# Equal distances for tile 0's lent banks, and two token groups of batch 1's q loaded after its v

**Chip, cores, metric.** One core of a Trainium2 chip. The metric is device time in microseconds (us) of one execution; lower is better. All runs named here are at a granted TensorE clock of 0.992 to 1.0.

## The reference, cut to what matters

An efficient attention feeds a two-layer network with a sine in the middle. Everything is f32 at the interface.

```python
q_s = softmax(q, axis=-1)                      # q, k, v: (8 batches, 8 heads, 576 tokens, 64)
k_s = softmax(k, axis=2)                       # over the tokens
kv  = einsum('bhsd,bhse->bhde', k_s, v)
x   = einsum('bhsd,bhde->bhse', q_s, kv)       # -> (4608 tokens, 512)
h   = x @ w_in                                 # (512, 2048)
g   = h + sin(alpha * h)**2 / alpha
out = g @ w_out                                # (2048, 512)
```

## The kernel before

The network runs over nine tiles of 512 tokens; attention of batch b + 1 is laid between the matmuls of tile b. PE is TensorE, DVE is VectorE, ACT is ScalarE, POOL is GpSimd, SP is SyncE, which issues most DMAs. One batch is 576 tokens, kept as J = 9 groups of 64, so tile 1 needs batch 0's last group and seven groups of batch 1; groups 7 and 8 of batch 1 belong to tile 2. In the listings `kvp` is the product of k and v in PSUM, `kbd` the same after its normalization, `xp` the attention output in PSUM and `xT` its bf16 copy, the network's input; the norm of q is a sum, a reciprocal and a product (`qs`, `qn`), and `o` is an output block on its way out.

The first layer's output for one of 16 column blocks (ni) stands in a PSUM bank until ACT has taken its sine and DVE has combined the two. There are four banks for that (`ps_h`), and tile 0 borrows two more from the attention's pool (`wide`):

```python
elif wide and (ni in (4, 5, 9, 10, 14, 15) if t == 0 else ni % 6 in (4, 5)):
    hp = wide()                     # a lent bank
else:
    hp = ps_h.tile([128, MF], F32, name="hp", tag="h")
```

Between tile 0's second layer and tile 1, batch 1 is prepared (cut; `take(os, n)` lets n matmuls of tile 0's second layer go by, four of its 64 also copy out an output block):

```python
take(os, 46)
exp_to(A["qe", 0][:, 8:9], staged["q", 0][:, :, 8:9])
exp_q(1)
load("v", v, 1, halves=True)
load_batch(2)
norm_q8(); norm_q(1, [GP, V]); exp_k(1)
# ... transposes of q (PE), two copies of them (DVE) ...
cast_v(1, [ACT_CP, DVE_CP])                    # f32 -> bf16, half on ACT, half on DVE
nc.scalar.activation(zero, zero, AX.Sin)       # switches ACT's table from Exp to Sin
take(os, 6)
# ... small xp of batch 0's last group; DVE copies it to xT ...
take(os, 2); kv_mm(1, 0, ps_e, split=True); kv_norm(1, 0, 1)
take(os, 2); kv_mm(1, 1, ps_e, split=True); kv_norm(1, 1, 2)
take(os, 1)
# ... xp and its copy to xT for batch 1's groups 0 to 6, then take(os) and tile 1 ...
```

In tile 1's second layer, batch 2 is prepared. SP issues here: the output block's two writes (inside `take`), batch 3's v, then two DMA transposes of batch 2's q.

```python
exp_q(2); exp_k(2)
os = o_stream(1)
take(os, 8)
# ... xp of batch 1's groups 7 and 8, DVE copies it to xT ...
take(os, 8)                          # first output block: DVE copies, SP writes it in two DMAs
norm_q(2, [GP, V])
exp_q(3); exp_k(3)
load("v", v, 3)
q_transpose_dma(2, halves=True)
# ... take(os, 16), kv of batch 2, take(os, 20) ...
# xp of batch 2 (needs the transposed q), tile 2
```

The softmax here doesn't subtract the row's maximum and nothing guards it: scores larger than these inputs give would overflow.

Of the kernel before, what the change touches and what calls it, by code (L numbers as in the profile page):

```python
# [15 lines left out]
F32 = mybir.dt.float32  # L16
BF16 = mybir.dt.bfloat16
AX = mybir.ActivationFunctionType
# [5 lines left out]
def kernel(  # L24
# [40 lines left out]
    ident = singles.tile([128, 128], F32, name="ident")  # L65
    identb = singles.tile([128, 128], BF16, name="identb")
    xT = singles.tile([128, 4, NT], BF16, name="xT")
    win = singles.tile([128, 4, d_ff], BF16, name="win")
    wout = singles.tile([128, nN, dm], BF16, name="wout")
    alpha_rows = singles.tile([nN, 128], F32, name="alpha_rows")  # L70
# [5 lines left out]
    def src_view(t, b):  # L76
        return t[b].rearrange("(i e) (p j) d -> (e p) i (j d)", e=2, j=J)
# [7 lines left out]
    def load(name, t, b, halves=False, eng=nc.sync, gate=None):  # L85

        st = stage.tile([128, 4, J, D], F32, name=f"st_{name}", tag="st")
        for ii in range(2) if gate else ():
            gate(st[:, ii, 0, 0:1], zero)
        view = src_view(t, b)  # L90
        flat = st.rearrange("p i j d -> p i (j d)")
        if halves:
            for ii in range(2):
                eng.dma_start(out=flat[:, ii::2], in_=view[:, ii::2])
        else:
            eng.dma_start(out=flat, in_=view)
        staged[name, b] = st

    def load_batch(b):
        load("q", q, b)  # L100
        load("k", k, b)
        load("v", v, b)
# [6 lines left out]
    def load_wout(c):  # L109
        nc.gpsimd.dma_start(out=wout[:, 4 * c:4 * c + 4, :], in_=wout_v[:, 4 * c:4 * c + 4, :])  # L110
# [4 lines left out]
    def exp_to(dst, src, iis=range(2)):  # L115
        for ii in iis:
            nc.scalar.activation(dst[:, :, ii * 128:(ii + 1) * 128].rearrange("p j (x d) -> p x j d", x=2),  # L117
                                 src[:, ii::2], AX.Exp)

    def exp_q(b):  # L120
        A["qe", b] = att2.tile([128, J, 4 * D], BF16, name="qe")
        exp_to(A["qe", b], staged["q", b])

    def exp_half(name, b, ii, j1=J):
        if ii == 0:
            A[name + "e", b] = att2.tile([128, J, 4 * D], BF16, name=name + "e")
        exp_to(A[name + "e", b][:, 0:j1], staged[name, b][:, :, 0:j1], (ii,))
# [5 lines left out]
    def cast_v(b, engs):  # L133
        vv = vb[b % 2].rearrange("p j (i c) -> p i j c", i=4)
        for ii in range(2):
            engs[ii](vv[:, 2 * ii:2 * ii + 2, :, 0:D], staged["v", b][:, ii::2])  # L136

    def norm_q(b, engs, j1=J):

        qe = A["qe", b][:, 0:j1].rearrange("p j (ii x d) -> p ii j x d", ii=2, x=2)  # L140
        A["qn", b] = qn = att1.tile([128, 2, J, 2 * D], BF16, name="qn")
        qs = small.tile([128, J, 4], F32, name="qs")
        if len(engs) == 1:
            nc.vector.tensor_reduce(qs, A["qe", b].rearrange("p j (i d) -> p j i d", i=4), axis=AXL.X, op=ALU.add)  # L144
            nc.vector.reciprocal(qs, qs)  # L145
        for ii in range(2):
            part = qs[:, 0:j1, 2 * ii:2 * ii + 2]
            if len(engs) == 2:
                nc.vector.tensor_reduce(part, qe[:, ii], axis=AXL.X, op=ALU.add)  # L149
                nc.vector.reciprocal(part, part)  # L150
            engs[ii % len(engs)].tensor_tensor(qn[:, ii, 0:j1].rearrange("p j (x d) -> p j x d", x=2), qe[:, ii],  # L151
                                               part.unsqueeze(3).to_broadcast([128, j1, 2, D]), op=ALU.mult)

    def norm_q8():

        qe = A["qe", 0][:, 8].rearrange("p (i d) -> p i d", i=4)
        qs = small.tile([128, J, 4], F32, name="qs")[:, 0]
        nc.vector.tensor_reduce(qs, qe, axis=AXL.X, op=ALU.add)
        nc.vector.reciprocal(qs, qs)
        nc.vector.tensor_tensor(qe, qe, qs.unsqueeze(2).to_broadcast([128, 4, D]), op=ALU.mult)  # L160

    def kv_mm(b, ii, pool, split=False):

# [22 lines left out]
    def q_tile(b):  # L186
        if ("qT", b) not in A:
            A["qT", b] = att2.tile([128, 2, J, 128], BF16, name="qT")
        return A["qT", b]

    def q_transpose(b, ii, pool, eng):
        tp = pool.tile([128, 16, 128], BF16, name="tp", tag="a")
        q_transpose_ii(b, ii, 0, J, tp)
        eng(q_tile(b)[:, ii], tp[:, 0:J])

    def q_transpose_ii(b, ii, j0, j1, tp):

        for j in range(j0, j1):
            nc.tensor.transpose(tp[:, j - j0], A["qn", b][:, ii, j], identb)
# [35 lines left out]
    def mm_h(t, ni, wide=None, k0=0, k1=4):  # L235

        if ni == 0 and k0 == 0:
            G[t] = gpool.tile([128, nN, MF], BF16, name="g")
        if k0:
            hp = HP[t, ni]  # L240
        elif wide and (ni in (4, 5, 9, 10, 14, 15) if t == 0 else ni % 6 in (4, 5)):
            hp = wide()
        else:
            hp = ps_h.tile([128, MF], F32, name="hp", tag="h")
        HP[t, ni] = hp
        for ki in range(k0, k1):
            nc.tensor.matmul(hp, win[:, ki, ni * 128:(ni + 1) * 128],  # L247
                             xT[:, ki, t * MF:(t + 1) * MF], start=(ki == 0), stop=(ki == 3))
        return hp
# [138 lines left out]
    def take(it, n=1000):  # L388
        for _ in range(n):
            if next(it, 0) == 0:  # L390
                return
# [4 lines left out]
    with ES:  # L396
        def lent():
            return ps_e.tile([128, 2, MF], F32, name="hh", tag="a")[:, 0]

        def load_q8():  # L400
            for ii in range(2):
                load0(nc.sync, "q", q, ii, 8, 9)

        late = {4: load_q8, 6: lambda: load("q", q, 1, halves=True, gate=DVE_CP), 8: lambda: load_wout(2),
                10: lambda: load_wout(3), 13: lambda: load("k", k, 1, halves=True, gate=DVE_CP)}
        for ni in range(nN):
            h_slot(0, ni, "DPPAPPAPPPAPPAPP"[ni], lag, lent)
            flush(lag, 1)
            if ni in late:
                late[ni]()  # L410
        flush(lag, 0)

        accs = [ps_h.tile([128, dm], F32, name="hp", tag="h") for _ in range(4)]
        os = o_quad(0, accs, [DVE_CP, ACT_CP, DVE_CP, ACT_CP])
        take(os, 46)
        exp_to(A["qe", 0][:, 8:9], staged["q", 0][:, :, 8:9])
        exp_q(1)
        load("v", v, 1, halves=True)
        load_batch(2)
        norm_q8()  # L420
        norm_q(1, [GP, V])
        exp_k(1)
        q_transpose(1, 0, ps_e, DVE_CP)
        tp = ps_e.tile([128, 16, 128], BF16, name="tp", tag="a")
        q_transpose_ii(1, 1, 0, J, tp)
        for ii in range(2):
            nc.tensor.transpose(tp[:, J + ii], A["qe", 0][:, 8, ii * 128:(ii + 1) * 128], identb)
        DVE_CP(A["qT", 1][:, 1], tp[:, 0:J])
        DVE_CP(A["qT", 0][:, :, 8], tp[:, J:J + 2])
        cast_v(1, [ACT_CP, DVE_CP])  # L430
        nc.scalar.activation(zero, zero, AX.Sin)
        take(os, 6)
        xp = ps_e.tile([128, 4, P], F32, name="xp", tag="a")
        for c in range(4):
            attn_chunk(0, c, 8, 9, xp[:, c])
        DVE_CP(xT[:, :, 8 * P:9 * P], xp)  # L436
        take(os, 2)
        kv_mm(1, 0, ps_e, split=True)
        kv_norm(1, 0, 1)
        take(os, 2)  # L440
        kv_mm(1, 1, ps_e, split=True)
        kv_norm(1, 1, 2)
        take(os, 1)

        c0 = J * P
        for ii in range(2):
            xp = ps_e.tile([128, 2, 512], F32, name="xp", tag="a")[:, :, 0:7 * P]
            for e in range(2):
                attn_chunk(1, 2 * ii + e, 0, 7, xp[:, e])
            (ACT_CP, DVE_CP)[ii](xT[:, 2 * ii:2 * ii + 2, c0:c0 + 7 * P], xp)  # L450
            take(os, 2)
        take(os)
        load("q", q, 3)
        load("k", k, 3)

        for ki in range(2):
            for ni in range(2):
                mm_h(1, ni, lent, ki, ki + 1)
        for ni in range(nN):
            h_slot(1, ni, SQ[ni], lag, lent)  # L460
            flush(lag, 1)
        cast_v(2, [GP_CP, GP_CP])
        flush(lag, 0)
# [16 lines left out]
    exp_k(2)  # L480
    os = o_stream(1)
    take(os, 8)
    xp = ps_a.tile([128, 4, 2 * P], F32, name="xp", tag="a")
    for c in range(4):
        attn_chunk(1, c, 7, 9, xp[:, c])
    DVE_CP(xT[:, :, (J + 7) * P:2 * J * P], xp)
    take(os, 8)
    norm_q(2, [GP, V])
    exp_q(3)
    exp_k(3)  # L490
# [107 lines left out]
```

## Time and profile before

| what | value | from |
|---|---|---|
| time | 289.31 us median of 4 (289.15 to 289.55) | the runs |
| span in the trace | 287.7 us | the profile |
| PE busy | 273.6 us, 95% | busy shares |
| PE's waits for other engines between 15 and 80 us that are listed | 0.7 + 0.7 + 0.3 us | list of waits |
| tile 1's first layer starts | 47.95 us | timeline |
| tile 1's second layer, start to tile 2's first matmul | 61.76 to 78.33, 16.57 us | timeline |

A matmul of 512 columns is recorded with 379 ns, but the next starts 216 ns later; the records overlap. A wait below about 0.16 us is therefore not seen as idle, and the end of one stage is best read as the start of the next. I compare stages by the starts of their first matmuls. Tile 2's start (start, duration, engine, line, operation):

```profile
78.33 3.62 PE L247 MATMUL hp<-xT,win 128*128 128x512 bf16 x15
```

### The profile page before, as it was taken

What the parts mean: (1) busy time and instruction counts of PE and PEld (TensorE: products, weight loads), DVE (VectorE), ACT (ScalarE), POOL (GpSimd) and SP (SyncE); (2) the same over time, 40 slices, a digit from 0 to 9 for tenths busy, and PEclk for the clock granted to TensorE, in tenths of its full rate; (3) what the DMA queues carried; (4) which work ended last, traced back from release to release, by engine and by line L of the source; (5) the groups of instructions that cost most, each with busy time, mean ns of one, the idle gap of its engine ahead of it and who ended that gap; (6) DMA issues with size and microseconds to landing.
All of it is one profiled execution on the core that took longest, in us unless ns stands there. A gap on an engine that the chain in (4) does not pass through costs nothing.

```text
span 287.7 us, 4238 instructions
## 1 busy us (share of the span) xinstructions
PE 273.6 (95%) x1541; PEld 131.3 (46%) x1569; DVE 189.2 (66%) x285; ACT 226.0 (79%) x319; POOL 81.8 (28%) x77
## 2 busy tenths in 40 slices
PE   2898998999999999999999999999999999999995
PEld 1444454445454445444544454444444444444443
DVE  4957966889958667856776676747674555555412
ACT  4978755999479999899889988998877777777500
POOL 2969420675775571005300440022000000000000
PEclk9999999999999999999999999999999999999999
DMA  7999999935899957129910991115111111111142
GB/s 260 311 200 247 264 395 407 309 150 166 190 181 402 371 185 126 38 45 375 265 34 22 328 311 29 38 39 131 24 39 36 36 36 39 36 36 38 40 109 73
DMA packets 38053, 45.77 MB, mean 159 GB/s; under 512 B 16512, under 2 KB 21392, under 8 KB 38032
## 3 DMA queue, kind: packets, MB, share of 16 engines
q1 hardware_dynamic: 32848, 40.57, 46.2%
q0 software_dynamic: 4992, 4.79, 9.6%
q8 instruction: 12, 0.20, 0.3%
q10 hardware_dynamic: 192, 0.14, 0.2%
q14 instruction: 9, 0.07, 0.1%
HBM read 36.71 MB, written 9.44 MB: 160 GB/s over the span
## 4 chain that ended last, share of the span: by engine, by line
PE 76%; DMA 9%; DVE 5%; ACT 3%; POOL 3%; issue 3%; SPq 0%; POOLq 0%; DVEq 0%; ACTq 0%
PE hp L247 34%; PE op L267 30%; DMA qT<-qn 4%; DMA st_v<-in_v_dram 4%; PE hh L247 2%; PE kvp L170 2%; PE xp L219 2%; POOL qn L151 1%; POOL s L257 1%; ACT s L253 1%; PE warm L328 1%; DMA st_q<-in_q_dram 1%; PE op L568 1%; PE op L247 1%; DVE qs L144 1%
## 5 line engine op out<-in xcount | busy, mean ns | idle before, releaser
L263 DVE SCALAR_TENSOR_TENSOR g<-s,inva_sb,hp 128x512 bf16<-128x512 f32 x130 | 96.3, 746 | 64.4 <-ACT s L255 54.5
L247 PE MATMUL hp<-xT,win 128*128 128x512 bf16 x512 | 129.0, 379 | 0.5
L267 PE MATMUL op<-wout,g 128*128 128x512 bf16 x479 | 121.8, 379 | 1.1 <-issue 0.5
L253 ACT ACTIVATE s<-hp,alpha_sb 128x512 f32<-128x512 f32 x130 | 87.7, 682 | 27.4 <-PE hp L247 25.1
L247 PEld LDWEIGHTS <-win 128*128 128x128 bf16 x576 | 56.2, 98 | 68.2 <-issue 1.2
L267 PEld LDWEIGHTS <-g 128*128 128x128 bf16 x560 | 54.1, 98 | 61.4 <-issue 0.6
L255 ACT ACTIVATE s<-s 128x512 f32<-128x512 f32 x111 | 69.9, 630 | 3.5
L151 POOL TENSOR_TENSOR qn<-qe,qs 128x1152 bf16<-128x1152 bf16 x12 | 25.3, 2127 | 72.3 <-DVE qs L145 62.7
L257 POOL TENSOR_TENSOR s<-s 128x512 f32<-128x512 f32 x30 | 31.5, 1060 | 25.8 <-ACT s L253 25.4
L273 DVE COPY o<-op 128x512 f32<-128x512 f32 (+2 forms) x33 | 22.1, 669 | 9.5 <-PE op L267 5.5
L117 ACT ACTIVATE ke<-st_k 128x1152 bf16<-128x1152 f32 x16 | 17.9, 1151 | 5.1 <-DMA st_k<-in_k_dram 5.1
L117 ACT ACTIVATE qe<-st_q 128x1152 bf16<-128x1152 f32 (+2 forms) x18 | 18.0, 1047 | 2.2 <-DMA st_q<-in_q_dram 1.9
L144 DVE TENSOR_REDUCE qs<-qe 128x36 f32<-128x2304 bf16 x5 | 12.8, 2553 | 8.7 <-ACT qe L117 8.6
L136 POOL CAST vb<-st_v 128x1152 bf16<-128x1152 f32 x12 | 13.6, 1162 | 10.6 <-DMA st_v<-in_v_dram 10.6
L267 PE MATMUL hp<-wout,g 128*128 128x512 bf16 x62 | 14.7, 379 | 0.2 <-issue 0.2
L222 DVE CAST xT<-xp 128x512 bf16<-128x512 f32 (+1 forms) x18 | 13.4, 743 | 0.0
L170 PEld LDWEIGHTS <-ke 64*128 64x128 bf16 x288 | 8.6, 95 | 5.6 <-issue 2.7
L170 PE MATMUL kvp<-vb,ke 64*128 64x130 bf16 x288 | 10.1, 219 | 1.0 <-DVE xT L436 0.7
L247 PE MATMUL hh<-xT,win 128*128 128x512 bf16 x39 | 9.4, 379 | 0.7 <-DVE g L263 0.7
L117 ACT ACT_TABLE_LOAD x7 | 9.0, 1283 | 1.3 <-PEq L582 1.2
L149 DVE TENSOR_REDUCE qs<-qe 128x18 f32<-128x1152 bf16 (+1 forms) x6 | 7.7, 1286 | 1.8 <-ACT qe L117 1.8
L219 PE MATMUL xp<-qT,kbd 128*128 128x256 bf16 (+1 forms) x40 | 8.2, 286 | 0.6 <-DVE xT L222 0.3
(76 smaller groups left out, 119.1 us busy)
## 6 DMA issues: line engine op xcount, KB each, us to landing
out_dram<-o SPq DMA_DIRECT2D x70, 128.0 KB, 2.3
st_q<-in_q_dram SPq DMA_DIRECT2D x6, 1152.0 KB, 6.6
st_k<-in_k_dram SPq DMA_DIRECT2D x6, 1152.0 KB, 8.6
st_v<-in_v_dram SPq DMA_DIRECT2D x6, 1152.0 KB, 10.3
st_k<-in_k_dram SPq DMA_DIRECT2D x4, 576.0 KB, 7.3
wout<-in_moe_w_out_dram POOLq DMA_DIRECT2D x4, 512.0 KB, 12.3
st_v<-in_v_dram SPq DMA_DIRECT2D x3, 576.0 KB, 9.9
win<-in_moe_w_in_dram POOLq DMA_DIRECT2D x6, 256.0 KB, 7.4
```

Of the source, the lines that this page charges most:

```text
L117: nc.scalar.activation(dst[:, :, ii * 128:(ii + 1) * 128].rearrange("p j (x d) -> p x j d", x=2), src[:, ii::2], AX.Exp)
L144: nc.vector.tensor_reduce(qs, A["qe", b].rearrange("p j (i d) -> p j i d", i=4), axis=AXL.X, op=ALU.add)
L151: engs[ii % len(engs)].tensor_tensor(qn[:, ii, 0:j1].rearrange("p j (x d) -> p j x d", x=2), qe[:, ii], part.unsqueeze(3).to_broadcast([12 ...
L170: nc.tensor.matmul(kvp[:, e, ii * 130:(ii + 1) * 130], ke[r, j, ii * 128:(ii + 1) * 128], vt[r, j, ii * 130:(ii + 1) * 130], start=(j == 0 ...
L219: nc.tensor.matmul(xp[:, e, 0:n], kt[:, e, ii], qT[:, ii, j0:j1, e * 64:(e + 1) * 64], start=True, stop=True)
L247: nc.tensor.matmul(hp, win[:, ki, ni * 128:(ni + 1) * 128], xT[:, ki, t * MF:(t + 1) * MF], start=(ki == 0), stop=(ki == 3))
L253: nc.scalar.activation(s, hp, AX.Sin, scale=alpha_sb[:, ni:ni + 1])
L255: nc.scalar.activation(s, s, AX.Square)
L257: nc.gpsimd.tensor_tensor(s, s, s, op=ALU.mult)
L263: nc.vector.scalar_tensor_tensor(G[t][:, ni], in0=s, scalar=inva_sb[:, ni:ni + 1], in1=hp, op0=ALU.mult, op1=ALU.add)
L267: nc.tensor.matmul(acc, G[t][:, ni, j * 128:(j + 1) * 128], wout[:, ni, :], start=(ni == 0), stop=(ni == nN - 1))
L273: eng(o[:, cols], acc)
```

## The change

The intent: take away tile 0's wait at its last lent bank by spacing the loans evenly, and let batch 1's v land earlier, by loading only the seven groups of q that tile 1 needs ahead of it. The rest of q goes behind v (`q78`) and is transposed and multiplied in tile 1's second layer.

```diff
-        elif wide and (ni in (4, 5, 9, 10, 14, 15) if t == 0 else ni % 6 in (4, 5)):
+        elif wide and ni % 6 in ((2, 3) if t == 0 else (4, 5)):
 ...                                   (load_q1: q's first load brings groups 0 to 6 only)
-        exp_q(1)
+        for ii in range(2):
+            exp_half("q", 1, ii, 7)
         load("v", v, 1, halves=True)
+        nc.sync.dma_start(out=q78.rearrange("p i j d -> p i (j d)"), in_=src_view(q, 1)[:, :, 7 * D:J * D])
         load_batch(2)
 ...                                   (transposes: seven groups instead of nine)
-        cast_v(1, [ACT_CP, DVE_CP])
-        nc.scalar.activation(zero, zero, AX.Sin)
         take(os, 6)
 ...                                   (small xp and its copy)
-        take(os, 2)
+        cast_v(1, [ACT_CP, DVE_CP])
+        exp_to(A["qe", 1][:, 7:J], q78)
+        nc.scalar.activation(zero, zero, AX.Sin)
+        take(os, 3)
         kv_mm(1, 0, ps_e, split=True)
         kv_norm(1, 0, 1)
-        take(os, 2)
+        take(os, 3)
 ...
         take(os)
+        norm_late(1, 7)
 ...                                   (in tile 1's second layer)
     take(os, 8)
+    tp = ps_a.tile([128, 2, 2, 128], BF16, name="tp", tag="a")
+    for ii in range(2):
+        for j in range(2):
+            nc.tensor.transpose(tp[:, ii, j], A["qe", 1][:, 7 + j, ii * 128:(ii + 1) * 128], identb)
+    DVE_CP(A["qT", 1][:, :, 7:J], tp)
+    take(os, 6)
     xp = ps_a.tile([128, 4, 2 * P], F32, name="xp", tag="a")
 ...
-    take(os, 8)
+    take(os, 2)
     norm_q(2, [GP, V])
```

More of the change, by code (lines that the diff above doesn't have):

```diff
@@ L67 @@
     xT = singles.tile([128, 4, NT], BF16, name="xT")
+    q78 = singles.tile([128, 4, 2, D], F32, name="q78")
     win = singles.tile([128, 4, d_ff], BF16, name="win")
@@ L152, in norm_q, with norm_late @@
                                                part.unsqueeze(3).to_broadcast([128, j1, 2, D]), op=ALU.mult)
-    def norm_q8():
-        qe = A["qe", 0][:, 8].rearrange("p (i d) -> p i d", i=4)
-        qs = small.tile([128, J, 4], F32, name="qs")[:, 0]
+    def norm_late(b, j0):
+        qe = A["qe", b][:, j0:J].rearrange("p j (i d) -> p j i d", i=4)
+        qs = small.tile([128, J, 4], F32, name="qs")[:, j0:J]
         nc.vector.tensor_reduce(qs, qe, axis=AXL.X, op=ALU.add)
         nc.vector.reciprocal(qs, qs)
-        nc.vector.tensor_tensor(qe, qe, qs.unsqueeze(2).to_broadcast([128, 4, D]), op=ALU.mult)
+        nc.vector.tensor_tensor(qe, qe, qs.unsqueeze(3).to_broadcast([128, J - j0, 4, D]), op=ALU.mult)
     def kv_mm(b, ii, pool, split=False):
@@ L402, in load_q8, with load_q1 @@
                 load0(nc.sync, "q", q, ii, 8, 9)
-        late = {4: load_q8, 6: lambda: load("q", q, 1, halves=True, gate=DVE_CP), 8: lambda: load_wout(2),
+        def load_q1():
+            staged["q", 1] = st = stage.tile([128, 4, J, D], F32, name="st_q", tag="st")
+            for ii in range(2):
+                DVE_CP(st[:, ii, 0, 0:1], zero)
+            for ii in range(2):
+                nc.sync.dma_start(out=st[:, ii::2, 0:7].rearrange("p i j d -> p i (j d)"),
+                                  in_=src_view(q, 1)[:, ii::2, 0:7 * D])
+        late = {4: load_q8, 6: load_q1, 8: lambda: load_wout(2),
                 10: lambda: load_wout(3), 13: lambda: load("k", k, 1, halves=True, gate=DVE_CP)}
@@ L416 @@
         exp_to(A["qe", 0][:, 8:9], staged["q", 0][:, :, 8:9])
-        exp_q(1)
+        for ii in range(2):
+            exp_half("q", 1, ii, 7)
         load("v", v, 1, halves=True)
+        nc.sync.dma_start(out=q78.rearrange("p i j d -> p i (j d)"), in_=src_view(q, 1)[:, :, 7 * D:J * D])
         load_batch(2)
-        norm_q8()
-        norm_q(1, [GP, V])
+        norm_late(0, 8)
+        norm_q(1, [GP, V], 7)
         exp_k(1)
-        q_transpose(1, 0, ps_e, DVE_CP)
-        tp = ps_e.tile([128, 16, 128], BF16, name="tp", tag="a")
-        q_transpose_ii(1, 1, 0, J, tp)
+        q_tile(1)
         for ii in range(2):
-            nc.tensor.transpose(tp[:, J + ii], A["qe", 0][:, 8, ii * 128:(ii + 1) * 128], identb)
-        DVE_CP(A["qT", 1][:, 1], tp[:, 0:J])
-        DVE_CP(A["qT", 0][:, :, 8], tp[:, J:J + 2])
-        cast_v(1, [ACT_CP, DVE_CP])
-        nc.scalar.activation(zero, zero, AX.Sin)
+            tp = ps_e.tile([128, 16, 128], BF16, name="tp", tag="a")
+            q_transpose_ii(1, ii, 0, 7, tp)
+            if ii == 1:
+                for i2 in range(2):
+                    nc.tensor.transpose(tp[:, 8 + i2], A["qe", 0][:, 8, i2 * 128:(i2 + 1) * 128], identb)
+            DVE_CP(A["qT", 1][:, ii, 0:7], tp[:, 0:7])
+        DVE_CP(A["qT", 0][:, :, 8], tp[:, 8:10])
         take(os, 6)
@@ L482 @@
     take(os, 8)
+    tp = ps_a.tile([128, 2, 2, 128], BF16, name="tp", tag="a")
+    for ii in range(2):
+        for j in range(2):
+            nc.tensor.transpose(tp[:, ii, j], A["qe", 1][:, 7 + j, ii * 128:(ii + 1) * 128], identb)
+    DVE_CP(A["qT", 1][:, :, 7:J], tp)
+    take(os, 6)
     xp = ps_a.tile([128, 4, 2 * P], F32, name="xp", tag="a")
```

## The prediction

> **What bounds the kernel now.** I read the page first (busy shares, the chain), then the list of waits of PE (TensorE), then the timeline around each place that the diff touches.
>
> ```profile
> PE 273.6 (95%) x1541; PEld 131.3 (46%) x1569; DVE 189.2 (66%) x285; ACT 226.0 (79%) x319; POOL 81.8 (28%) x77
> ...
> PE 76%; DMA 9%; DVE 5%; ACT 3%; POOL 3%; issue 3%; SPq 0%; POOLq 0%; DVEq 0%; ACTq 0%
> ```
>
> PE is busy for 95% of the span and carries 76% of the chain. The kernel can only get shorter where PE stands still, so I look for those places. The list of PE's waits (us in total, times, longest) has three in the stretch that changes:
>
> ```profile
> PE kvp L170 <- DVE xT L436: 0.7, 1, 0.7
> PE hh L247 <- DVE g L263: 0.7, 1, 0.7
> ...
> PE kvp L170 <- ACT vb L136: 0.3, 1, 0.3
> ```
>
> Their sum, 1.7 us or 0.6% of 289.29 us, is a rough ceiling for what the change aims at. The timeline of that stretch:
>
> ```profile
> 27.02 1.41 DVE L263 SCALAR_TENSOR_TENSOR g<-s,inva_sb,hh 128x512 bf16<-128x512 f32 x2 [1.06 <-POOL s L257]
> ...
> 27.83 1.89 PE L247 MATMUL hh<-xT,win 128*128 128x512 bf16 x8 [0.68 <-DVE g L263]
> ...
> 41.64 1.17 ACT L136 CAST vb<-st_v 128x1152 bf16<-128x1152 f32 x1 [0.20 <-DMA st_v<-in_v_dram]
> ...
> 42.83 1.28 ACT L431 ACT_TABLE_LOAD   x1
> ...
> 43.09 0.77 DVE L136 CAST vb<-st_v 128x1152 bf16<-128x1152 f32 x1 [1.29 <-DMA st_v<-in_v_dram]
> ...
> 44.37 0.41 DVE L436 CAST xT<-xp 128x256 bf16<-128x256 f32 x1
> ...
> 44.84 0.69 PE L170 MATMUL kvp<-vb,ke 64*128 64x130 bf16 x18 [0.75 <-DVE xT L436]
> ...
> 46.26 0.91 ACT L450 CAST xT<-xp 128x896 bf16<-128x896 f32 x1 [1.46 <-PE xp L227]
> ...
> 47.95 3.62 PE L247 MATMUL hp<-xT,win 128*128 128x512 bf16 x16
> ```
>
> Batch 1's v lands in two halves, at 41.6 and 43.07. The DVE cast of the second stands ahead of the copy of xp (L436), whose PSUM buffer the second kvp needs: so v's landing holds PE to 44.84, and from there PE runs solid until tile 1 starts at 47.95. The third place is the second linear layer of tile 1, where four transposes go now:
>
> ```profile
> 61.76 1.89 PE L267 MATMUL op<-wout,g 128*128 128x512 bf16 x7
> ...
> 64.27 0.75 DVE L263 SCALAR_TENSOR_TENSOR g<-s,inva_sb,hp 128x512 bf16<-128x512 f32 x1 [0.41 <-POOL s L257]
> ...
> 64.93 0.68 DVE L486 CAST xT<-xp 128x512 bf16<-128x512 f32 x1
> ...
> 65.64 0.69 DVE L273 COPY o<-op 128x512 f32<-128x512 f32 x1
> 66.25 1.34 DVE L149 TENSOR_REDUCE qs<-qe 128x18 f32<-128x1152 bf16 x1
> ```
>
> Here DVE is the tight engine: the reductions of batch 2's q queue behind its copies, the q then goes through a DMA transpose (in the chain: 71.71, 3.78 us), and PE takes the result at 75.53, some 0.28 us after its preceding matmul (75.03 + 0.22 + a small hand-over). That wait is almost hidden, but it has no slack left.
>
> **What the Trainium skill says.** (1) "DMA: Bandwidth & Descriptors", section "Queues, rings and completion order": each DMA engine alternates between the queues that have work. The packet records agree: between 34.5 and 36.5 us some 45 packets of the GpSimd queue (wout) and 45 of the SyncE queue start per 0.5 us. One engine drains wout last, at 39.56, and the landing of v waits for that engine. (2) The same page, "Why small descriptors are slow (HBM only)", gives about 3 cycles of overhead per packet of 32-byte beats, so a 512-byte packet costs 19 cycles against 75 for 2304 bytes, a quarter. The records show 18 ns for 256 bytes, 84 for 2048 and 93 for 2304, so I take 25 ns for 512 and 73 for 1792 bytes (estimates). (3) "ScalarE: Activation LUTs", "What ACT_TABLE_LOAD costs": about 1283 ns a switch; the trace has 1283 ns. The further 1380 ns of drain it speaks of doesn't show: at 42.83 the load starts 0.02 us after the cast.
>
> **The change part by part.**
>
> *Lent banks.* Tile 0 used six lent PSUM tiles at ni 4, 5, 9, 10, 14, 15, so ni 14 reuses the one of ni 9 after five steps; now (2, 3, 8, 9, 14, 15) every reuse is six steps apart. ni 14 then waits for the combine of 8 (done about 25.96), and 15 for that of 9 (27.78). PE would reach ni 14 at 27.22 (15.11 + 14 x 0.865) and the 0.61 us to 27.83 go. But ACT's last sines wait for their four s buffers, not for PE (the sine of 13 at 27.87 waited for DVE's combine 9), so ACT, DVE and the exp of q keep their times. PE only arrives 0.6 us earlier at work whose inputs come by DMA.
>
> *The loads.* Of q(1), 7/9 (32 packets an engine of 1792 instead of 2304 bytes) go ahead of k and v: 32 x (90 - 73) = 0.54 us less on the late engine. v lands at about 41.05 and 42.5. The rest (q78, 32 packets of 512 bytes, 0.8 us) lands at about 43.3, near where v ended before.
>
> *Batch 1 on PE.* 46 matmuls from 28.95 to 38.9; 16 transposes at 0.057 us to 39.8; six matmuls and the small xp to 41.3; three matmuls to 41.9; first kvp from 42.3 (ACT's cast ends 41.07 + 1.17 = 42.24) to 42.86; three matmuls, second kvp 43.5 to 44.06 (DVE's cast 42.55 to 43.32, now behind the xp copy, so that wait is gone); one matmul, xp, two, xp, two, one: PE could be done at about 46.1, against 47.95.
>
> *ACT takes over.* Exp of q78 stands after the cast and before the Sin table. It waits for 43.3, costs 2 x 0.40 less overlap = 0.75 (128 elements take 0.293, 1152 take 1.155 us, so 256 take 0.40), to 44.05; table 1.28 to 45.33; the dummy sine 0.2, the o copy 0.57, the xT copy 0.91, each overlapping by 0.05 to 0.09: 46.9. Tile 1 starts at about 46.9, 1.0 us earlier than before, and 0.8 us short of what PE alone would allow.
>
> *The late norm.* 128x512: reduction 0.64, reciprocal 0.18, multiply about 0.75: 1.6 us of DVE, after its xT copy and before the first combine of tile 1. That gap was 2.58 us: hidden.
>
> *Tile 1's second layer,* counted from its start T (61.76 before). DVE's last combine ends at T + 3.17. New behind it: the copy of the four transposes, 512 elements, 0.40 us (256 take 0.28, 1152 take 0.76), to T + 3.58. PE (eight matmuls, transposes 0.23, six matmuls) is at xp at T + 3.26 and stands 0.38 us. xp, 0.22, and its PSUM latency: the xT copy runs from T + 4.02 to 4.70, the o copy to 5.39, the reduction starts at about T + 5.3 instead of T + 4.49. So batch 2's norm, its DMA transposes and the landing go back by 0.8 us. PE needs them 0.23 + 0.38 = 0.61 us later than before, so it waits about 0.2 us more than the 0.28. In all this phase is 0.8 us longer, of which 0.23 is moved transposes (saved in batch 1 already).
>
> Sum: -1.0 + 0.8 = -0.2 us; from tile 2 on everything is as before, shifted. 289.29 - 0.2 = 289.1.
>
> **Rivals.** *Full gain:* if the q78 exp costs nothing on the path (an early landing) and DVE absorbs the extra copy, PE starts tile 1 at 46.1 and loses only 0.23 in tile 1: -1.6 us, 287.7. For it: PE's own work ends there. Against it: ACT's sum above, and no idle DVE between 64.27 and 69. *q78 late:* if 512-byte packets take 41 ns (the mean of 16 such in the alpha load), q78 lands 0.5 us later, ACT hands over at 47.4, and with the 0.8 the kernel takes 289.5. *A worse pile-up:* the DMA transposes of batch 2 move on to collide with v(3) and output writes, adding perhaps 0.5 us: 289.8. Against it: v(3)'s issue hangs on the same o copy and moves along. *DMA-hidden banks:* the bank part alone is worth 0, since the landing of v, not PE, sets 44.84; this is in my sum.
>
> **Range and chances.** The terms are uncertain by about 0.5 us each (q78's landing, DVE's delay), runs by 0.2 us: 288.3 to 289.9. Two per cent is 5.8 us, over three times all the PE waits in this stretch, so faster or slower than that needs something outside the trace: 0.01 each, same 0.98.
>
> **What would show it.** Right: the 0.68 wait at tile 0's last lent tile gone; the wait of kvp for L436's copy gone; ACT's exp of q78 waiting for its DMA until about 43.3; PE waiting about 0.8 us for ACT's xT copy and tile 1 starting near 46.9; in tile 1's second layer the reduction at T + 5.3 and the phase 17.4 us long instead of 16.57 (61.76 to 78.33). Wrong: tile 1 starting at 47.5 or later (q78 late), or the reduction not delayed (then 288.3), or PE waits beyond 80 us that are not there now.

## The result

The changed kernel took 290.30 us (median of 4, 290.05 to 290.88) against 289.31: ratio 1.0036, 95% interval 1.0019 to 1.0054. Ratios are computed as the mean time of one kernel's fast runs over that of the other's of the same rounds, so they are not quite the ratio of the medians quoted. In the sense of the 2% classes the two are the same, but the change is a small loss, 1.0 us, outside the predicted range of 288.3 to 289.9.

The page of the changed kernel, busy shares and chain by engine:

```profile
PE 275.9 (96%) x1569; PEld 131.5 (46%) x1569; DVE 190.2 (66%) x289; ACT 226.1 (78%) x321; POOL 81.4 (28%) x77
...
PE 80%; DMA 6%; ACT 4%; DVE 4%; issue 2%; POOL 2%; SPq 0%; ACTq 0%
```

These say nothing of the loss: PE's share even rises. (The x1541 of before and the x1569 here are not more work; some matmul records are missing from the trace of before.) PE's list of waits is what moved:

```profile
PE hp L228 <- DMA qT<-qn: 1.5, 1, 1.5
...
PE hp L248 <- ACT xT L464: 0.3, 1, 0.3
...
PE xp L228 <- DVE qT L502: 0.2, 1, 0.2
```

The three waits of before that the change aimed at are gone. In their place stand a short one for ACT's xT copy, one for the copy of the new transposes, and one of 1.5 us for the DMA transposes of batch 2. The timeline where batch 1 ends (start, duration, engine, line, operation, in brackets the idle time before and what ended it):

```profile
43.09 0.72 ACT L118 ACTIVATE qe<-q 128x256 bf16<-128x256 f32 x2 [1.02 <-DMA q<-in_q_dram]
43.83 1.28 ACT L450 ACT_TABLE_LOAD   x1
...
45.70 0.91 ACT L464 CAST xT<-xp 128x896 bf16<-128x896 f32 x1
...
46.66 3.61 PE L248 MATMUL hp<-xT,win 128*128 128x512 bf16 x16 [0.32 <-ACT xT L464]
```

This is the predicted hand-over from q78 through ACT to PE. Tile 1 starts at 46.66 instead of 47.95, so the first half of the change gained 1.29 us. Then tile 1's second layer:

```profile
60.47 1.89 PE L268 MATMUL op<-wout,g 128*128 128x512 bf16 x8
...
63.64 0.42 DVE L502 COPY qT<-tp 128x512 bf16<-128x512 bf16 x1
64.11 0.38 PE L228 MATMUL xp<-qT,kbd 128*128 128x128 bf16 x4 [0.23 <-DVE qT L502]
...
65.74 1.34 DVE L150 TENSOR_REDUCE qs<-qe 128x18 f32<-128x1152 bf16 x1
...
75.45 0.32 PE L228 MATMUL hp<-qT,kbd 128*128 128x384 bf16 x1 [1.51 <-DMA qT<-qn]
...
79.27 3.62 PE L248 MATMUL hp<-xT,win 128*128 128x512 bf16 x16
```

It starts at 60.47 and tile 2's first matmul comes at 79.27: 18.80 us instead of 16.57. So 2.23 us are lost where 0.8 were predicted, and the account closes: -1.29 + 2.23 = +0.94 us at tile 2, against +0.9 us of span (288.6 - 287.7). The reduction stands at T + 5.27, T being the layer's start, just where it was predicted. The excess must come between the reduction and the transposed q. The norm in that stretch isn't longer than before: SP issues the transposes at T + 9.24, against T + 8.46, which is the predicted shift. What is left is SP's queue. What SP issued before the change (start, duration, line, DMA, how many):

```profile
66.36 1.11 SPq L276 DMA_DIRECT2D out_dram<-o  x2
67.57 0.53 SPq L96 DMA_DIRECT2D st_v<-in_v_dram  x1
...
70.22 3.39 SPq L209 DMA_TRANSPOSE qT<-qn  x2
```

and after it:

```profile
65.85 2.11 SPq L277 DMA_DIRECT2D out_dram<-o  x2
68.06 0.53 SPq L97 DMA_DIRECT2D st_v<-in_v_dram  x1
...
69.71 4.63 SPq L210 DMA_TRANSPOSE qT<-qn  x2
```

Taken singly, the second of the two output writes took 1.59 us to issue, where it took 0.60 before. Batch 3's v, next in SP's order, is issued 1 us late, and the transposes stand in the same queue behind v's data: v's packets run from 69.28 to 73.92 (68.79 to 72.95 before), those of the transposes to 75.97 (75.00 before). What was next to the slow issue? The DMA queues in the window from 66 to 67.7 us, changed kernel (queue and kind: packets, MB, share of the 16 engines):

```profile
q1 hardware_dynamic: 75, 0.12, 31.5%
q8 instruction: 1, 0.02, 5.0%
```

One packet of 16 KB on the instruction queue, from 66.24 to 67.59 by the packet records. In the kernel before, the window from 66 to 67.7 has none; there that packet came at 62.76 to 63.69, while SP issued nothing:

```profile
q8 instruction: 1, 0.02, 3.9%
```

The Trainium skill, "Runtime: NRT & Kernel Launch", section "Instruction fetch mechanics", says that each engine's instruction memory is refilled in blocks of 16 KiB, 256 instructions, and that the cost of crossing a block is mostly hidden. There are 12 such packets in the run and PE's program has 3157 instructions, 12.3 blocks; between one packet and the next PE runs 251 recorded instructions on the mean in the changed kernel (195 to 316). So I take them for PE's refills; that they are PE's is inferred from these counts.

**Theory.** The predicted part of the change is right. The rest of the loss, 1.5 us, is a collision: the change moved an instruction fetch from a place where SP was idle to one where SP issues the output writes; the issue waits for the fetch, and v and the transposes are behind it. **Rivals:** DVE's delay alone sets the landing; the lent banks lose something; it was chance, or one chip.

### The profile page after: what moved, and what is told of

It is laid out like the page before. It is cut to its first block, busy times and chain, and to the rows that moved or that the text cites. A ratio compares the mean times of both kernels' runs of the same rounds, so it can differ in the third digit from the quotient of the medians.

```text
span 288.6 us, 4275 instructions
## 1 busy us (share of the span) xinstructions
PE 275.9 (96%) x1569; PEld 131.5 (46%) x1569; DVE 190.2 (66%) x289; ACT 226.1 (78%) x321; POOL 81.4 (28%) x77
## 4 chain that ended last, share of the span: by engine, by line
PE 80%; DMA 6%; ACT 4%; DVE 4%; issue 2%; POOL 2%; SPq 0%; ACTq 0%
PE hp L248 36%; PE op L268 33%; DMA q<-in_q_dram 4%; PE hh L248 2%; PE kvp L171 2%; ACT s L254 2%; POOL s L258 2%; DMA qT<-qn 2%; PE xp L220 2%; PE warm L329 1%; DMA st_q<-in_q_dram 1%; PE op L589 1%; PE op L248 1%; DVE qs L150 1%; DVE g L264 1%
## 5 line engine op out<-in xcount | busy, mean ns | idle before, releaser
L268 PE MATMUL op<-wout,g 128*128 128x512 bf16 x496 | 124.4, 379 | 0.0
L152 POOL TENSOR_TENSOR qn<-qe,qs 128x1152 bf16<-128x1152 bf16 (+1 forms) x12 | 24.9, 2091 | 73.0 <-DVE qs L146 63.4
L118 ACT ACTIVATE qe<-st_q 128x1152 bf16<-128x1152 f32 (+3 forms) x18 | 17.6, 1024 | 2.2 <-DMA st_q<-in_q_dram 2.1
L118 ACT ACT_TABLE_LOAD x7 | 9.0, 1283 | 1.3 <-PEq L603 1.2
L150 DVE TENSOR_REDUCE qs<-qe 128x16 f32<-128x1024 bf16 (+2 forms) x6 | 7.2, 1197 | 2.0 <-ACT qe L118 2.0
```

Of the source, the lines that this page charges most:

```text
L118: nc.scalar.activation(dst[:, :, ii * 128:(ii + 1) * 128].rearrange("p j (x d) -> p x j d", x=2), src[:, ii::2], AX.Exp)
L152: engs[ii % len(engs)].tensor_tensor(qn[:, ii, 0:j1].rearrange("p j (x d) -> p j x d", x=2), qe[:, ii], part.unsqueeze(3).to_broadcast([12 ...
L268: nc.tensor.matmul(acc, G[t][:, ni, j * 128:(j + 1) * 128], wout[:, ni, :], start=(ni == 0), stop=(ni == nN - 1))
```

## The experiments

Twelve kernels, each with five rounds and a profile, in three series of four; all were correct. The kernel before ran beside each series: medians 289.54 (11 runs), 289.58 (12, the former eleven and one more) and 289.26 (11). The table has what matters of the profiled run of each; the columns are the instruction fetch near the writes, the longer of the two output-write issues, the length of tile 1's second layer (start to tile 2's first matmul), and the time.

| kernel | fetch, us | issue | layer | median | ratio to before, 95% |
|---|---|---|---|---|---|
| before (first trace) | 62.76-63.69 | 0.60 | 16.57 | 289.31 | |
| changed (first trace) | 66.24-67.59 | 1.59 | 18.80 | 290.30 | 1.0036 (1.0019-1.0054) |
| banks_only | from 62.96 | 0.60 | 16.74 | 289.43 | 1.0004 (0.9977-1.0032) |
| v3_early | 65.13-66.34 | 0.78 | 16.86 | 288.93 | 0.9977 (0.9960-0.9993) |
| cols_late | 65.22-66.39 | 1.09 | 17.19 | 288.76 | 0.9975 (0.9958-0.9992) |
| tiny12 | from 61.05 | 0.60 | 17.30 | 289.47 | 0.9997 (0.9979-1.0014) |
| changed_again | 66.55-67.85 | 1.72 | 19.22 | 290.86 | 1.0039 (1.0016-1.0062) |
| tiny6 | from 61.64 | 0.60 | 17.60 | 289.48 | 0.9998 (0.9977-1.0019) |
| v3_and_cols | 65.50-66.70 | 0.76 | 16.56 | 288.72 | 0.9972 (0.9956-0.9989) |
| before_v3 | from 62.45 | 0.59 | 16.25 | 289.06 | 0.9994 (0.9967-1.0022) |
| before_tiny12 | from 61.92 | 0.60 | 16.57 | 289.34 | 0.9999 (0.9982-1.0016) |
| late_only | 66.15-67.43 | 1.56 | 18.83 | 290.59 | 1.0042 (1.0025-1.0059) |
| before_less5 | 66.10-67.52 | 0.92 | 17.17 | 290.37 | 1.0033 (1.0004-1.0061) |
| before_less12 | 66.72-67.64 | 1.39 | 17.96 | 291.45 | 1.0071 (1.0046-1.0095) |

**banks_only**: the kernel before with only the new places of the lent banks.

```diff
-        elif wide and (ni in (4, 5, 9, 10, 14, 15) if t == 0 else ni % 6 in (4, 5)):
+        elif wide and ni % 6 in ((2, 3) if t == 0 else (4, 5)):
```

> The kernel before with only the new places of tile 0's lent banks. My theory: the 0.68 us wait of PE at ni 14 goes, PE gets to batch 1 0.6 us earlier and waits there for v, whose landing is set by DMA; tile 1 still starts at about 47.9 us, time within 0.1 us of before (ratio 1.000). Rival: the 0.6 us reach the end, 288.7 us (ratio 0.998).

289.43 against 289.54: nothing that the runs can see. The interval is wide here (one run took 291.37) and just holds the rival's 0.998 too, so the trace has to decide. PE's waits show where the gain went:

```profile
PE kvp L170 <- ACT vb L136: 0.9, 1, 0.9
PE kvp L170 <- DVE xT L436: 0.7, 1, 0.7
...
PE hp L267 <- DMA wout<-in_moe_w_out_dram: 0.3, 1, 0.3
```

The wait at tile 0's last bank is gone, the one for v's cast grew from 0.3 to 0.9 us, and a wait of 0.3 us for the last part of w_out is new. Tile 1 started at 48.23 in this trace. Here, being early at work that waits for a transfer was worth nothing.

**v3_early**: the changed kernel, batch 3's v issued as soon as its buffer is free, ahead of the output writes.

```diff
     exp_q(2)
+    load("v", v, 3)
     exp_k(2)
 ...
     exp_k(3)
-    load("v", v, 3)
```

> The changed kernel with batch 3's v issued ahead of the two output writes of tile 1, as soon as the exps of batch 2's q have freed its buffer. Theory A: what holds PE for 1.5 us at 75.45 is that the DMA transposes of batch 2 stand behind batch 3's v on the same queue; issued 2.5 us earlier v is through by about 71.5, the transposes land by 74, the wait falls under 0.4 us and the kernel takes about 288.7 us (ratio to before 0.998). Rival B: DVE's later norm alone sets the landing; then the wait stays at 1.3 us or more and the time near 290.2.

288.93 us, and PE has no listed wait for the transposes any more. SP's issues:

```profile
65.31 0.37 SPq L97 DMA_DIRECT2D st_v<-in_v_dram  x1
65.98 1.41 SPq L277 DMA_DIRECT2D out_dram<-o  x2
69.84 2.83 SPq L210 DMA_TRANSPOSE qT<-qn  x2
```

v's packets are through at 71.02 instead of 73.92. DVE's reduction is as late as in the changed kernel (65.87 against a layer start of 60.61), so DVE's delay alone, rival B, doesn't make the wait: the queue behind v does. A fetch lies here too, but it holds only a write, behind which nothing urgent stands.

**cols_late**: the changed kernel, with the late transposes and the small xp moved behind batch 2's norm.

```diff
-    take(os, 8)
-    (transposes, copy, take 6, xp, copy, take 2)
+    take(os, 16)
 ...
     kv_norm(2)
+    (transposes into a ps_h bank, copy)
+    take(os, 16)
+    (xp into a ps_h bank, copy)
     norm_q(3, [GP])
-    take(os, 20)
+    take(os, 4)
```

> The changed kernel with the four late transposes, the copy of them, the small xp and its copy moved behind batch 2's norm, in ps_h banks. Theory A (DMA queue order, started by DVE's delay): the reduction starts about 1.5 us earlier after the start of tile 1's second layer (T + 3.9 instead of T + 5.3), so output copy, v's issue and transposes all come earlier; PE's wait at the transposes falls below 0.5 us, the kernel takes about 288.7 us. If the late v issue came from something else (an instruction fetch next to the output write), v is issued with 1 us of delay all the same and a wait of about 1 us stays: 289.5.

288.76 us. The reduction stands at T + 4.35 (65.06 - 60.71), 0.9 us earlier after T than in the changed kernel and not the 1.5 that I had expected, because DVE now waits for PE's output block. The write's issue is again stretched, but to 1.09 us and not 1.59, and v is issued at T + 6.16 instead of T + 7.59; the transposes hold PE for 0.19 us only. This run lessens DVE's delay and the slow issue together, so it doesn't tell them apart. The others do: DVE's delay without the slow issue leaves at most 0.3 us of listed wait at the transposes (none in tiny12, 0.3 in tiny6), and the slow issue without DVE's delay makes one of 1.3 us (before_less12).

**tiny12**: the changed kernel with twelve matmuls of one column at a place where PE waits anyway. They give PE 24 instructions more and change nothing else.

```diff
     kv_mm(0, 1, ps_e, split=True)
+    for _ in range(12):
+        nc.tensor.matmul(warm[:, 0, 0:1], identb, identb[:, 0:1], start=True, stop=True)
```

> The changed kernel with 12 matmuls of one column in a place at 13.6 us where PE waits 1.0 us for DVE: they shift where PE's instruction stream is by 24 instructions and cost nothing in time. In the changed kernel a 16 KB instruction fetch at 66.24 (62.76 before) falls together with the second output write, whose issue took 1.59 us instead of 0.60. If that fetch makes the 1 us, and the place in PE's stream sets its time, the fetch comes some 2.5 us earlier, the issue takes 0.6 us again, v is issued at about 67.1 and the kernel takes about 289.3 us. If the fetch has nothing to do with it: issue again 1.6 us and 290.3.

289.47 us, 0.83 under the first median of the changed kernel and, in the next series, 1.4 under its second. The fetch came at 61.05, the issue took 0.60 us, and the layer 17.30 us, where the prediction had 17.4; PE has no listed wait for the transposes:

```profile
66.09 1.11 SPq L277 DMA_DIRECT2D out_dram<-o  x2
67.30 0.54 SPq L97 DMA_DIRECT2D st_v<-in_v_dram  x1
69.95 3.10 SPq L210 DMA_TRANSPOSE qT<-qn  x2
```

**changed_again**: the changed kernel once more, unedited, beside the next three.

> The changed kernel as it is, beside the next three on one chip. If the loss of 1 us is of the kernel and not of one chip or one series: 290.2 to 290.5 us, the instruction fetch again at about 66.2, the second output write's issue again 1.6 us, tile 2 starting near 79.3. If it was chance: within 0.3 us of before, tile 2 starting near 78.1.

290.86 us, ratio 1.0039: the loss is of the kernel. The fetch met the write again (issue 1.72 us), and tile 2 started at 79.82. One of its six runs took 289.62, so an execution may escape.

**tiny6**: as tiny12 with six.

```diff
-    for _ in range(12):
+    for _ in range(6):
```

> The changed kernel with six one-column matmuls in place of twelve. Fetch theory: the fetch moves by half as much, to between 62.5 and 65, clear of the output writes at 65.9 to 66.9; the issue takes 0.6 us, v is issued at about 67.2, and the time is that of tiny12, 0.8 us under the changed kernel beside it. If the twelve gained by something else than the fetch (a warmer PE, other start), six gain half, 0.4 us.

289.48 us, the time of tiny12 and not half its gain. The fetch moved more than I expected, to 61.64, nearly as far as with twelve, so its place goes in jumps. The layer took 17.60 us, with 0.3 us of waiting for the transposes that tiny12 doesn't have, so it varies by that much without a fetch at the writes. Since 12 and 24 more instructions give the same time, the number of small matmuls isn't what gains.

**v3_and_cols**: both repairs (the two diffs above, together).

> Both moves at once: batch 3's v ahead of the output writes, and the late columns behind batch 2's norm. PE had waits of 0.19 and about 0.3 us left at the transposes in the one, 0.23 and 0.2 us before the small xp in the other; with both, all of these go: about 0.3 to 0.5 us under either alone, 288.4 us.

288.72 us, the lowest median of all. The gain over either repair alone (0.04 to 0.2 us) is below the noise, less than I expected. The waits at the transposes and at the small xp are gone from PE's list and the layer takes 16.56 us. In its profiled run tile 1 started only at 47.38, with 0.6 us of waiting for v's cast, so the first half varies too.

**before_v3**: the kernel before with the diff of v3_early.

> The kernel before with batch 3's v issued ahead of the output writes, nothing else. Theory A: only the wait of 0.28 us at the transposes can go, 0.2 to 0.3 us (ratio 0.999), so most of what that move gives to the changed kernel is a repair of what the change broke. Rival: the move is worth 1 us by itself, then 288.4 us.

289.06 us, ratio 0.9994 with an interval from 0.9967 to 1.0022 (one of six runs took 291.33). The layer shrank by 0.32 us as expected. It isn't told apart from before, nor from the two repaired kernels with certainty: v3_and_cols is 0.3 us lower by the medians, and its ratio interval lies below 1.

**before_tiny12**: the control, the small matmuls in the kernel before (the diff of tiny12).

> Control: the twelve one-column matmuls in the kernel before, where no fetch meets the output writes. Fetch theory: nothing to gain, time as before (ratio 0.999 to 1.001), issue of the second output write 0.60 us. If the small matmuls gain by themselves (what they gave the changed kernel would then not be the fetch): 0.8 us less, 288.8 us.

289.34 us, ratio 0.9999. The small matmuls gain nothing by themselves.

**late_only**: the changed kernel with the old places of the banks (the first diff, reversed).

> The changed kernel with the lent banks where they were in the kernel before. My theory: the banks are worth nothing in time because PE waits for v's landing or for ACT's xT copy afterwards; PE waits 0.7 us at tile 0's ni 14 again, tile 1 starts near 46.7 all the same, and the time is that of the changed kernel, 290.3 to 290.9, if the fetch meets the writes again. Rival: the banks carry part of the loss or gain: off by 0.5 us or more at the same place of the fetch.

290.59 us, ratio 1.0042, like the changed kernel's 1.0036 and 1.0039. PE waits its 0.7 us in tile 0, tile 1 starts at 46.54 all the same, the fetch meets the write. In neither surrounding are the banks worth anything that the runs can tell from noise (about 0.5 us here). This series ran on chip 5 and the two before it on chip 15, so the loss isn't of one chip either.

**before_less5** and **before_less12**: the counter-test. The kernel before, without five or all twelve of its warm-up matmuls, so that its fetch comes later.

```diff
-    warm_up(7)        (less12 only)
-    warm_up(2)
-    warm_up(3)
```

> Counter-test: the kernel before without five of its warm-up matmuls (the groups of two and three), so ten instructions fewer ahead. Fetch theory, if the place in PE's stream sets the fetch: it moves from 62.8 towards 64 to 66. Only where it meets the output writes at 66.3 to 67.5 does their issue get longer than 0.6 us, and then v, the transposes and the end come 0.5 to 1 us later (290.0 to 290.5). If it doesn't reach them, the time stays within 0.3 us of before.

> The same with all twelve warm-up matmuls taken out: 24 instructions fewer, the fetch towards 66 to 68. If it meets the writes, issue over 1 us, PE waiting over 1 us at the transposes, 290.0 to 291; if not, as before, apart from what a cold PE costs at the start, which the wait for v at 43 to 45 us should hide. If the issue is long without a fetch beside it, or short with one, the fetch theory falls.

The collision could be made in the kernel before. Without five the fetch came at 66.10, the issue took 0.92 us, PE waited 0.5 us for the transposes, and the time was 290.37 (289.14 to 291.84: here executions differ). Without twelve, the issue took 1.39 us; PE's waits and SP's issues of that run:

```profile
PE hp L227 <- DMA qT<-qn: 1.3, 1, 1.3
```

```profile
66.11 1.91 SPq L276 DMA_DIRECT2D out_dram<-o  x2
68.12 0.53 SPq L96 DMA_DIRECT2D st_v<-in_v_dram  x1
69.97 4.56 SPq L209 DMA_TRANSPOSE qT<-qn  x2
```

That is the picture of the changed kernel, without any of the change: DVE's reduction stands at T + 4.48, as before (T + 4.49), so the slow issue alone makes the wait. PE is slower at the start without its warm-up matmuls (two matmuls of 512 columns at 12.5 us took 1.06 us, where they took 0.59 at 12.3 before). This cost about 1 us early (the second layer of tile 0 began at 30.45 instead of 29.55), and v's landing hid it: tile 1 started at 47.70. The median, 291.45, is more than the collision of the profiled run explains (that run took 290.29, the least of the six), and what the other five lost in addition isn't known.

**One more look at all traces.** In every trace where a fetch overlaps the issue of these two writes with effect (changed, changed_again, late_only, before_less5, before_less12, cols_late, v3_early, v3_and_cols), the long issue ends 0.37 to 0.42 us after the fetch's packet ends. It is no matter of one place: the first load of batch 4 in the kernel before took 1.30 us to issue beside the fetch at 82.39, and ended 0.39 us after it. An issue that begins shortly before the fetch, or is the first inside it, often goes through at its usual 0.37 to 0.47 us (in before_less5 the first write did; but in banks_only a write at 46.62, the first beside the fetch of 46.61, took 1.24); the next one waits. So what these traces show is that the next issue of such a write completes about 0.4 us after the fetch does. A fetch isn't the only cause of a long issue: at 41.6 to 42.2 us an output write took 0.81 to 1.44 us to issue without one, in six of the traces (changed, changed_again, v3_early, cols_late, tiny6, v3_and_cols), while SP's queue moved about 410 GB/s of batch loads. A crowded queue doesn't explain the writes at 66 us: for at least 3.9 us before them no packet but the fetch's was under way, in any trace.

## Why the prediction was wrong

By its own steps:

- *Lent banks, worth 0*: right. banks_only and late_only show it, and the wait that takes the place is the predicted one, for v.
- *The loads*: right, with small offsets. ACT could cast v at 40.90 (41.05 predicted), DVE at 42.34, without waiting (42.5), exp of q78 began at 43.09 (43.3). Packets of 512 bytes took 27 ns, not the estimated 25 (0.29 of the 93 ns of 2304 bytes; the quarter that the prediction worked out from the page's overhead was an estimate too); those of 1792 took 75, not 73. The first half of v was ready 0.74 us earlier, not 0.54; the sum had put a packet of 2304 bytes at 90 ns that the prediction itself reads at 93, which is 0.1 of it.
- *Batch 1 on PE and ACT's take-over*: the mechanism was right, the size off. Tile 1 started at 46.66, 1.29 us earlier and not 1.0, mostly since q78 came 0.2 us earlier than estimated. PE waited for ACT's xT copy, as predicted, but 0.3 us by the list and not 0.8.
- *The late norm, hidden*: right. Its three parts took 0.69, 0.20 and 0.69 us after DVE's xT copy, and DVE still waited 1.55 us afterwards.
- *Tile 1's second layer, the reduction at T + 5.3*: right (T + 5.27). *The phase 0.8 us longer*: this is the step that failed, in its sentence "So batch 2's norm, its DMA transposes and the landing go back by 0.8 us". The norm and the issue of the transposes did go back by 0.8 (T + 9.24 against T + 8.46), but the landing, the end of their last packet, went back by 2.26 (T + 15.50 against T + 13.24). I took the way from the issue to the landing as fixed and only shifted. The rival "a worse pile-up" was dismissed with "v(3)'s issue hangs on the same o copy and moves along", and that is what didn't hold: v's issue came another 1 us later, because an instruction fetch fell on the write ahead of it. That rival had the place and the direction, at 0.5 us instead of 1.5, but not the fetch; none of the signs that the prediction listed for being wrong came. Without that fetch (tiny12) the layer took 17.30 us, 0.73 longer than before, against the predicted 0.8, and the kernel as a whole stood at 0.9997 of before.
- The size of the missing term: 18.80 - 17.30 = 1.50 us. The issue accounts for 0.99 (1.59 - 0.60); the passage of v's packets for about 0.53, being 4.64 us long instead of 4.11 in tiny12. Why v itself ran slower isn't shown.

The prediction's count from the traces was thus good to about 0.3 us on each stage, and its sum, a gain of 0.2 us, would have been near that of tiny12, 0.1 us (ratio 0.9997), which holds the change without the collision. What it didn't look at was a queue that no instruction of the kernel names. The fetches were visible before the change, as the line "q8 instruction" on the page.

Left open: what sets the moment of a fetch. It moved by 0.8 to 5.2 us for 10 to 24 instructions of PE, but also by about 1 us between the changed kernel and v3_early, whose order of PE's instructions is the same. And it isn't shown why the issue has to wait, only that it does.

Of the versions run, v3_and_cols (0.9972 of before) and its two halves (0.9977, 0.9975) have ratios to before whose intervals lie below 1; they are not told apart from each other. Each keeps the change and takes the fragile queue order away.

## What to carry to other kernels

Before you call a delay on a DMA path "only shifted", list everything that is ahead on its queue and on its issuing engine, and move the urgent transfer or its competitor so that neither an output write nor a bulk load stands ahead of it. When a small change makes a loss of about a microsecond that no instruction explains, look in the packet records for instruction fetches next to the slow DMA issue, and test it by adding a few instructions that cost no time: if the loss goes, it came from the place of the fetch and not from the edit's own work. And expect nothing from a wait removed ahead of a transfer that has not landed.

## What the Trainium skill lacked or had wrong

- "Runtime: NRT & Kernel Launch", section "Instruction fetch mechanics", calls the cost of crossing a 16 KiB block mostly hidden. Here PE, whose fetch it is by the counts, has no listed wait beside it, but another engine's DMA issue was held up: 1.59 us instead of 0.60, ending 0.37 to 0.42 us after the fetch, and the kernel lost about 1 us by it (290.3 against 289.5 with the fetch moved). The page doesn't mention effects on other engines' DMA issues.
- "ScalarE: Activation LUTs", section "What ACT_TABLE_LOAD costs": the 1283 ns of the load are exact here, but the drain of 1380 ns that it adds to each switch doesn't show: in the changed kernel the load began at 43.83, 0.02 us after the exp, and the dummy sine at 45.12, 0.01 us after the load.
